# w2 phi2 with VectorE block turns in place of TensorE flips in five of eight chunks, in an attention, MoE and soft-MoE kernel on one core

## The chip, the cores and the metric

The kernel runs as one launch on one NeuronCore of a Trainium2 chip. The metric is the device time of one execution in microseconds, as the median of the runs. TensorE (PE) multiplies, VectorE (DVE), ScalarE (ACT) and GpSimd (POOL) work on elements, and SyncE (SP) issues every transfer between device memory and SBUF. All data are fp32; a part of the large products reads operands rounded to fp32r, split into a high and a low part.

## The reference

Attention over 32 memory slots, then a mixture of experts (`x` becomes `_moe_ref(...)`), then a soft mixture of experts. Cut to what the change touches:

```python
def _moe_ref(x, domain_probs, w1, w2):          # N=2304, D=512, E=4, F=1024
    for e in range(E):
        h = np.maximum(x @ w1[e], 0.0)
        out += p[:, e:e + 1] * (h @ w2[e])
    return out

def _moe2_ref(x, phi, w1, w2):                  # 8 experts, 32 slots
    logits = x @ phi                            # phi: 512 x 32
    d = softmax(logits, axis=0)
    slot_input = d.T @ x
    ...
```

The kernel never forms the output of the first mixture. It needs the 32 logits of each token, and h @ w2[e] @ phi = h @ (w2[e] phi). So it computes M = w2 phi2 once: for each of 4 experts a 1024 x 32 matrix, with `phi2` the 512 x 32 matrix of the second mixture.

## The kernel before, in words

The work is listed as steps. Each step has an engine, a planned cost, what it reads and writes, and a place `at` on a common scale. A planner (`Plan.order`) plays the steps through with those costs and writes one fixed order for each engine. On the chip every engine then takes its own list from the front, and a step waits for what it reads and for the places it overwrites. A step that waits holds up all that stands behind it on its engine.

The four batches are done in units: three units with 576 tokens of 4 heads by 2 halves each, and two half units for the last batch. Within a unit TensorE does, for 8 chunks of w1 (expert e, half f), `g_mult` (L695, folding w1 with the attention's values), 8 blocks of `up` (6 products each, L770 to L772, into one of three PSUM banks), and `logits` (L806, with M). ScalarE applies Relu (L778), VectorE turns the result in 32 x 32 blocks (L784) and GpSimd scales it (L788). Beside this the attention of the next batch is prepared (`memory`, `query`: L464 to L657).

`m_chunk(n, ats)` computes M for chunk n, which is one half of one expert's w2, 512 rows of 512. It is called for n = 0 to 7, all during the first unit. In the text "chunk 1" is n = 0 and "chunk 8" is n = 7. For each chunk:

- one transfer of 1 MB brings 512 rows of w2 into place `R[3 + n % 2]`, in runs of 8 KB (four rows to a partition);
- TensorE flips it in four groups of four 128 x 128 blocks (`flip`, L837), into a bank of `g_bank()`, which has two (4 and 5); ScalarE (L847) and VectorE (L843) copy the groups to SBUF in turn;
- four products of 128 x 32 by 128 x 512 (`part`, L854) with `phi2_sb` as weights, a copy by ScalarE (L860), and four products with the folding matrix `si` (`fold`, L866), which add the four parts; VectorE copies the result to M (L871).

`g_mult` takes the same two banks and gives them back when VectorE has done L706. Chunks with even n and odd n take turns in two places in SBUF, so a chunk's transfer waits for the reads of the chunk two before it.

Late in the kernel two TensorE steps load weights in steps of four elements: `slots` (L1249, `part[:, c::4]`) and the flip of the second mixture's h (L1292, `hs.rearrange("s (p f) -> s f p", f=4)[:, a_]`). They are of the kind of L866 and of L837, which load theirs in one run.

All transfers are issued by SP in one list. They use eight semaphores in turn, so a transfer is issued when the one eight before it has landed.

Of the kernel before, what the change touches and what calls it, by code (L numbers as in the profile page):

```python
# [11 lines left out]
PE, ACT, DVE, POOL, SP = "PE", "ACT", "DVE", "POOL", "SP"  # L12


class Plan:
# [16 lines left out]
    def add(self, eng, cost, fn, r=(), w=(), at=0.0, size=0, lag=LAG):  # L32
        self.stages.append((at, len(self.stages), eng, cost, fn, tuple(r), tuple(w), size, lag))
# [163 lines left out]
def dve(n):  # L197
    return 0.15 + 0.00107 * n
# [138 lines left out]
def program(  # L337
    tc, const, swap, ps, q, k, v, phi, dprob, w1, w2, phi2, v1, v2, out, nc, B, H, S, HD, NM, E, D, F, NSLOT, FH, NCH, SCALE, NT, HB, NG, ident, si, rr, r1, rf, ind, phi2_sb, dp, dps, pe, pe2, ct, kb, vb, kbs, vbs, M, srun, mrun, zrun, small, lts, lrs, lcs, dts, R, RAW, GP, AT, HT, NHT, PH, KT, QB, QT, XB, NX, YB, NY, MX, END, uses, h3, hts, atts, zone, z0, at_place, swapped, bank, MM, LB, S0, plan, **_
):
    add = plan.add  # L340

    def wk(o, n):
        return key("W", o, o + n)

    def pk(n):
        return key("ps", n)
# [7 lines left out]
    def g_bank():  # L354
        return uses(S0, S0 + 1)
# [11 lines left out]
    def dma(to, of, size, r=(), w=(), at=0.0, cost=0.6):  # L367
        add(SP, cost, lambda: nc.sync.dma_start(  # L368
            out=to() if callable(to) else to, in_=of() if callable(of) else of,
        ), r=r, w=w, at=at, size=size)  # L370
# [448 lines left out]
            r=[("M", n)] + [wk(o, width) for o in hos], w=[pk(LB)], at=at, lag=0)  # L819


    def m_chunk(n, ats):
        e, f = divmod(n, F // FH)
        o = R[3 + n % 2]

        def wn():
            return at_place(o, 2048).rearrange("p (a d) -> p a d", a=4)

        def wt():
            return at_place(o + 2048, 2048).rearrange("p (c f) -> p c f", c=4)  # L830
        dma(wn(), w2[e, f * FH:f * FH + FH, :].rearrange("(j a) d -> j a d", a=4), 1048576, w=[wk(o, 2048)], at=ats[0])
        for a in range(4):
            bk = g_bank()

            def flip(a=a, bk=bk):
                for c in range(4):
                    nc.tensor.transpose(  # L837
                        bank[bk][:, 128 * c:128 * c + 128], wn()[:, a, 128 * c:128 * c + 128], ident
                    )
            add(PE, 0.42, flip, r=[wk(o + 512 * a, 512), "cst"], w=[pk(bk)], at=ats[1 + a])  # L840
            src = bank[bk].rearrange("p (c f) -> p c f", c=4)
            if a % 2:
                add(DVE, dve(512), lambda a=a, src=src: nc.vector.tensor_copy(  # L843
                    out=wt()[:, :, 128 * a:128 * a + 128], in_=src),
                    r=[pk(bk)], w=[("wt", n % 2, a)], at=ats[1 + a] + 0.1)
            else:
                add(ACT, act(512), lambda a=a, src=src: nc.scalar.copy(  # L847
                    out=wt()[:, :, 128 * a:128 * a + 128], in_=src),
                    r=[pk(bk)], w=[("wt", n % 2, a)], at=ats[1 + a] + 0.1)
        bk = g_bank()  # L850

        def part():
            for c in range(4):
                nc.tensor.matmul(  # L854
                    bank[bk][32 * c:32 * c + 32, :], phi2_sb[:, c, :], wt()[:, c], start=True, stop=True,
                )
        wtk = wk(o + 2048, 2048)
        add(PE, 0.9, part, r=[("wt", n % 2, a) for a in range(4)] + [wtk, "phi2"], w=[pk(bk)], at=ats[5])
        mp = ct[:, 0:512]
        add(ACT, act(512), lambda: nc.scalar.copy(out=mp, in_=bank[bk]), r=[pk(bk)], w=["mp"],  # L860
            at=ats[5] + 0.1)
        b2 = g_bank()

        def fold():
            for a in range(4):
                nc.tensor.matmul(  # L866
                    bank[b2][:, 32 * a:32 * a + 32], mp[:, 128 * a:128 * a + 128], si,
                    start=True, stop=True,
                )
        add(PE, 0.95, fold, r=["mp", "cst"], w=[pk(b2)], at=ats[6])  # L870
        add(DVE, 0.3, lambda: nc.vector.tensor_copy(  # L871
            out=M[:, 4 * n:4 * n + 4], in_=bank[b2][:, 0:128].rearrange("p (a s) -> p a s", a=4),
        ), r=[pk(b2)], w=[("M", n)], at=ats[6] + 0.1)
# [272 lines left out]
    for x in range(4):  # L1146
        bk = att_bank()
        add(PE, 0.3, lambda x=x, bk=bk: spread(x, bk), r=["dpn", "cst"], w=[pk(bk)], at=2.5 + x)
        add(DVE, 1.1 if x == 3 else 0.5, lambda x=x, bk=bk: tables(x, bk), r=[pk(bk)], w=["pe"], at=2.6 + x)

    m_at = [2.5, 6.2, 10.5, 14.5, 18.5, 22.5, 26.5, 30.5]
    for n, m0 in enumerate(m_at):
        m_chunk(n, [m_at[n - 2] + 1.6 if n > 1 else n - 181.5, m0, m0 + 0.5, m0 + 1, m0 + 1.5, m0 + 2.4, m0 + 3.2])

    def attention(b, base):
        load_phi(b, base + 1)
# [8 lines left out]
    for u, (b, ranges) in enumerate(units):  # L1165
        if b + 1 < B:
            attention(b + 1, starts[u])
        for n in range(NCH):
            s = b * NCH + n
# [30 lines left out]
    for e in range(2):  # L1200
        def turn_s(e=e):
# [6 lines left out]
            at=z + 0.1)  # L1208
        x = sts[:, e]
        src = bank[so_b[e]].rearrange("p (k s) -> p k s", k=8)  # L1210
        w = [("M", n) for n in range(NCH)] if e == 0 else [("sts", 1)]
        if e:
            add(DVE, dve(512), lambda x=x, src=src: nc.vector.tensor_copy(out=x, in_=src), r=[pk(so_b[e])] + [("M", 7)],
                w=[("sts", e)], at=z + 0.2)
        else:
            add(ACT, act(512), lambda x=x, src=src: nc.scalar.copy(out=x, in_=src), r=[pk(so_b[e])],
                w=[("sts", e)] + [("M", n) for n in range(NCH)], at=z + 0.2)
# [25 lines left out]
    part = at_place(PART, 512)  # L1243
# [3 lines left out]
    def slots():  # L1247
# [7 lines left out]
        out=sT, in_=bank[b1][:, 0:128].rearrange("p (c s) -> p c s", c=4)  # L1255
# [11 lines left out]
    for m in range(4):  # L1267
        bu = end_mm()
        zz = z + 3 + 2 * m
        for n in range(4):  # L1270
# [15 lines left out]
            out=hs, in_=bank[bu], func=ACTF.Relu, scale=rz,  # L1286
# [28 lines left out]
    for e in range(8):  # L1315
        for nn in range(2):
# [9 lines left out]
            at = zz + 0.1 * (2 * e + nn)  # L1326
# [7 lines left out]
    for n, ab in enumerate(accs):  # L1334
        so, sk = sos[n]
        at = zz + 0.75 + n
        add(ACT, act(256), lambda ab=ab, so=so: nc.scalar.copy(out=so[:, 0:256], in_=bank[ab][:, 0:256]),
            r=[pk(ab)], w=[("so", n, 0), sk], at=at)
# [33 lines left out]
    at = zz + 3  # L1372
# [52 lines left out]
```

## Time and profile before

| | us |
|---|---|
| median of 3 runs | 508.97 |
| the runs | 508.2, 508.97, 511.94 |
| profiled execution | 507.71 |
| its span (first to last instruction) | 505.9 |
| TensorE busy in the span | 476.3 (94%) |
| VectorE, ScalarE, GpSimd busy | 297.1, 202.7, 212.1 |

The times in the trace are counted from the span's start. "Busy" is the time in which an engine has at least one instruction under way. On TensorE the products overlap (their ends are modelled), so that a group's busy time is smaller than its count times the mean of one. The weight loads (PEld) overlap with the products.

### The profile page before, as it was taken

What the parts mean: (1) busy time and instruction counts of PE and PEld (TensorE: products, weight loads), DVE (VectorE), ACT (ScalarE), POOL (GpSimd) and SP (SyncE); (2) the same over time, 40 slices, a digit from 0 to 9 for tenths busy, and PEclk for the clock granted to TensorE, in tenths of its full rate; (3) what the DMA queues carried; (4) which work ended last, traced back from release to release, by engine and by line L of the source; (5) the groups of instructions that cost most, each with busy time, mean ns of one, the idle gap of its engine ahead of it and who ended that gap; (6) DMA issues with size and microseconds to landing.
All of it is one profiled execution on the core that took longest, in us unless ns stands there. A gap on an engine that the chain in (4) does not pass through costs nothing.

```text
span 505.9 us, 13222 instructions
## 1 busy us (share of the span) xinstructions
PE 476.3 (94%) x5592; PEld 338.2 (67%) x5592; DVE 297.1 (59%) x605; ACT 202.7 (40%) x475; POOL 212.1 (42%) x255
## 2 busy tenths in 40 slices
PE   3999999999999999999999999999999989999971
PEld 2677787777876788788668887775687866333230
DVE  6588546656685857767684676586677553100032
ACT  2354445555550555455245555433543330010031
POOL 0244224546651348775324778532773850000000
PEclk9999999999999999999999999999999999899996
DMA  7999866415420946362082645525345988999938
GB/s 223 235 352 315 331 173 204 153 34 179 165 85 4 319 118 185 106 188 84 3 265 86 205 168 179 197 85 195 97 130 202 356 302 328 412 426 419 421 127 332
DMA packets 65243, 106.08 MB, mean 210 GB/s; under 512 B 28576, under 2 KB 40864, under 8 KB 59552
## 3 DMA queue, kind: packets, MB, share of 16 engines
q1 hardware_dynamic: 65184, 105.23, 60.9%
q8 instruction: 44, 0.72, 0.6%
q14 instruction: 15, 0.12, 0.1%
HBM read 100.50 MB, written 4.72 MB: 208 GB/s over the span
## 4 chain that ended last, share of the span: by engine, by line
PE 78%; DMA 14%; SPq 3%; DVE 2%; ACT 1%; issue 1%; DVEq 0%; ACTq 0%
PE ps L770 15%; PE ps L771 13%; PE ps L772 13%; PE ps L976 8%; DMA v<-in_moe_w_dram 8%; PE ps L695 6%; PE ps L806 5%; DMA h<-in_moe_w_dram 3%; PE ps L837 3%; SPq L368 3%; DMA raw<-in_moe_w_dram 3%; PE ps L813 2%; PE ps L854 2%; PE ps L603 2%; PE ps L615 2%; PE ps L866 1%
## 5 line engine op out<-in xcount | busy, mean ns | idle before, releaser
L788 POOL TENSOR_TENSOR h<-h,pe 128x576 f32<-128x576 f32 (+1 forms) x160 | 157.7, 996 | 141.5 <-DVE h L784 117.6
L770 PE MATMUL ps<-A,g 128*128 128x288 f32 x512 | 158.0, 309 | 0.2 <-ACT hts L778 0.2
L778 ACT ACTIVATE hts<-ps 128x288 f32<-128x288 f32 x256 | 105.1, 412 | 130.4 <-PE ps L772 129.0
L771 PE MATMUL ps<-A,g 128*128 128x288 f32 x512 | 151.1, 295 | 0.0
L772 PE MATMUL ps<-A,g 128*128 128x288 f32 x512 | 150.9, 295 | 0.0
L784 DVE STREAM_TRANSPOSE h<-hts 128x576 f32<-128x576 f32 (+1 forms) x160 | 102.4, 647 | 53.5 <-ACT hts L778 53.0
L770 PEld LDWEIGHTS ps<-A,g 128*128 128x128 f32 x512 | 96.1, 188 | 23.9 <-issue 18.6
L771 PEld LDWEIGHTS ps<-A,g 128*128 128x128 f32 x512 | 96.2, 188 | 0.3 <-POOL A L657 0.2
L772 PEld LDWEIGHTS ps<-A,g 128*128 128x128 f32 x512 | 96.1, 188 | 0.0
L706 DVE TENSOR_TENSOR g<-ps,g 128x512 fp32r<-128x512 f32 x64 | 41.0, 678 | 20.0 <-ACT g L704 19.9
L704 ACT CAST g<-ps 128x512 fp32r<-128x512 f32 x64 | 34.9, 590 | 34.5 <-PE ps L695 33.8
L976 PE MATMUL ps<-h,dts 32*32 32x512 f32 x1152 | 40.0, 597 | 1.6 <-DVE dts L958 1.6
L695 PE MATMUL ps<-raw,vbs 64*32 64x512 f32 x512 | 35.9, 600 | 1.6 <-DVE g L706 0.9
L976 PEld LDWEIGHTS ps<-h,dts 32*32 32x32 f32 x1152 | 22.8, 103 | 15.2 <-issue 4.6
L806 PE MATMUL ps<-hts,M 128*32 128x288 f32 x384 | 28.2, 411 | 0.0
L632 POOL TENSOR_TENSOR atts<-atts,small 128x256 f32<-128x256 f32 (+1 forms) x20 | 11.5, 575 | 25.7 <-DVE small L630 25.6
L837 PE MATMUL ps<-ident,h 128*128 128x128 f32 x128 | 18.1, 278 | 0.2 <-DVE g L706 0.2
L806 PEld LDWEIGHTS ps<-hts,M 128*32 128x32 f32 x384 | 10.4, 109 | 10.6 <-issue 5.1
L643 POOL TENSOR_TENSOR atts<-atts,small 128x256 f32<-128x256 f32 (+1 forms) x20 | 11.5, 575 | 13.4 <-DVE small L641 6.3
L837 PEld LDWEIGHTS ps<-ident,h 128*128 128x128 f32 x128 | 14.5, 143 | 2.4 <-issue 1.4
L894 POOL TENSOR_TENSOR lts<-lts,pe 128x288 f32<-128x288 f32 x15 | 10.4, 691 | 12.6 <-DMA v<-in_moe_w_dram 9.4
L657 POOL TENSOR_TENSOR A<-atts,A 128x256 fp32r<-128x256 f32 (+1 forms) x20 | 13.6, 680 | 4.4 <-ACT A L655 4.4
(185 smaller groups left out, 508.6 us busy)
## 6 DMA issues: line engine op xcount, KB each, us to landing
raw<-in_moe_w_dram SPq DMA_DIRECT2D x32, 1024.0 KB, 5.2
v<-in_moe_w_dram SPq DMA_DIRECT2D x20, 1024.0 KB, 12.5
h<-in_moe_w_dram SPq DMA_DIRECT2D x18, 1024.0 KB, 8.4
h<-in_k_dram SPq DMA_DIRECT2D x8, 512.0 KB, 5.2
h<-in_v_dram SPq DMA_DIRECT2D x8, 512.0 KB, 7.1
atts<-in_moe_w_dram SPq DMA_DIRECT2D x4, 1024.0 KB, 9.0
atts<-in_q_dram SPq DMA_DIRECT2D x12, 256.0 KB, 5.6
atts<-in_phi_dram SPq DMA_DIRECT2D x8, 256.0 KB, 4.7
```

Of the source, the lines that this page charges most:

```text
L695: nc.tensor.matmul(bank[bs[c]][32 * i:32 * i + 32, :], vb[b % 2][64 * c:64 * c + 64, 32 * i:32 * i + 32], t()[64 * c:64 * c + 64, i, :], s ...
L704: add(ACT, act(512), lambda c=c, src=src: nc.scalar.copy(out=placed(g()[:, 2 * c]), in_=src), r=[pk(bs[c])], w=[wk(o + 1024 * c, 512)], at ...
L706: add(DVE, dve(512), lambda c=c, src=src: nc.vector.tensor_tensor(out=placed(g()[:, 2 * c + 1]), in0=src, in1=placed(g()[:, 2 * c].bitcast ...
L770: nc.tensor.matmul(t, gh, ah, start=(c == 0), stop=False)
L771: nc.tensor.matmul(t, gh, al, start=False, stop=False)
L772: nc.tensor.matmul(t, gl, ah, start=False, stop=(c == 1))
L778: add(ACT, act(w), lambda: nc.scalar.activation(out=t[:, o0 - base:o1 - base], in_=bank[bm][:, 0:w], func=ACTF.Relu,), r=[pk(bm)], w=[wk(h ...
L784: add(DVE, dve(width), lambda: nc.vector.transpose(out=h_of(u, e)[:, kx], in_=t), r=[wk(ho, width)], w=[hk], at=at + 0.4)
L788: add(POOL, pool(width), lambda: nc.gpsimd.tensor_tensor(out=h_of(u, e)[:, kx], in0=h_of(u, e)[:, kx], in1=share, op=ALU.mult), r=["pe"], ...
L806: nc.tensor.matmul(lb[r0:r0 + 32, 0:HB], M[:, 4 * n + a, :], at_place(hos[a] + o0, o1 - o0), start=(first and h == 0), stop=(not first and ...
L837: nc.tensor.transpose(bank[bk][:, 128 * c:128 * c + 128], wn()[:, a, 128 * c:128 * c + 128], ident)
L976: nc.tensor.matmul(bank[S0 + p][32 * c:32 * c + 32, :], dtv[rows, tb, :], h_pair(u, ep)[rows, :, :, tb, :], start=(tb < 2), stop=(tb >= nt ...
```

## The change

Chunks 1 to 3 (n < 3) stay as they were. For chunks 4 to 8, `m_turned` takes the place of `m_chunk`:

- w2's half expert comes in four transfers of 256 KB, each into 32 partitions. A partition then has 8 rows' pieces of 256 columns, in runs of 1 KB.
- VectorE turns it in 32 x 32 blocks, four instructions of 128 x 512, SBUF to SBUF.
- TensorE does 32 small products (64 x 32 weights from a second copy of phi2, 64 x 128 of the turned w2): for c = 0 to 7 one in each of four 64 x 32 tiles of the array, added over c in PSUM.
- One VectorE turn of 128 x 128 from PSUM writes M.

The columns that a small product streams are read from SBUF in the order a, x, y of the layout `(y a c h x)`: y is innermost, and its two values lie 4 KB apart.

The second copy of phi2 (`load_phi2`) is four transfers of 32 KB in runs of 128 bytes. The flips of chunks 1 to 3 name the new transfers' keys as read, which orders them before the new transfers. The cost that the planner is given for the 32 products is 2.3.

```diff
+    def load_phi2(at):
+        for p in range(4):
+            dh = p % 2
+            dma(
+                lambda p=p: phi_of()[32 * p:32 * p + 32],
+                phi2[256 * dh:256 * dh + 256].rearrange("(c i) s -> i c s", i=32),
+                32768, w=[("phi2", p)] + ([wk(R[4] + 4096, 256)] if p == 0 else []), at=at,
+            )
+    def m_turned(n, ats):
+        e, f = divmod(n, F // FH)
+        o = R[3 + n % 2]
...
+        def wt():
+            return at_place(o + 2048, 2048).rearrange("p (y a c h x) -> p h c a x y", y=2, a=4, c=8, h=2)
+        for p in range(4):
+            fh, dh = divmod(p, 2)
+            src = w2[e, FH * f:FH * f + FH, 256 * dh:256 * dh + 256]
+            src = src.rearrange("(h x k) d -> h x k d", h=2, k=8)[fh]
+            dma(
+                lambda p=p: wn(0, 4)[32 * p:32 * p + 32].rearrange("p (k d) -> p k d", k=8), src,
+                262144, w=[("wn", o, p)] + ([wk(o, 2048)] if p == 0 else []), at=ats[0] + 0.001 * p,
+            )
+        for a in range(4):
+            add(DVE, dve(512), lambda a=a: nc.vector.transpose(
+                out=at_place(o + 2048 + 512 * a, 512), in_=wn(a, 1)),
+                r=[wk(o + 512 * a, 512)] + [("wn", o, p) for p in range(4)],
+                w=[wk(o + 2048 + 512 * a, 512)], at=ats[1 + a])
+        bk = g_bank()
+        def part():
+            for c in range(8):
+                for q in range(4):
+                    rows = slice(64 * (q // 2), 64 * (q // 2) + 64)
+                    nc.tensor.matmul(
+                        bank[bk][32 * q:32 * q + 32, 0:128], phi_of()[rows, c, :], wt()[rows, q % 2, c],
+                        start=(c == 0), stop=(c == 7),
+                    )
+        add(PE, 2.3, part, r=[wk(o + 2048, 2048), wk(R[4] + 4096, 256)] + [("phi2", p) for p in range(4)],
+            w=[pk(bk)], at=ats[5])
+        add(DVE, 0.3, lambda: nc.vector.transpose(
+            out=M[:, 4 * n:4 * n + 4].rearrange("p a s -> p (a s)"), in_=bank[bk][:, 0:128],
+        ), r=[pk(bk)], w=[("M", n)], at=ats[5] + 0.1)
...
+    load_phi2(6)
     m_at = [2.5, 6.2, 10.5, 14.5, 18.5, 22.5, 26.5, 30.5]
     for n, m0 in enumerate(m_at):
-        m_chunk(n, [m_at[n - 2] + 1.6 if n > 1 else n - 181.5, m0, m0 + 0.5, m0 + 1, m0 + 1.5, m0 + 2.4, m0 + 3.2])
+        (m_chunk if n < 3 else m_turned)(n, [m_at[n - 2] + 1.6 if n > 1 else n - 181.5, m0, m0 + 0.5, m0 + 1, m0 + 1.5, m0 + 2.4, m0 + 3.2])
```

How the engines' lists stand at three places, with the line numbers of each kernel (L843, L871 and L891 of before are L897, L925 and L945 after). VectorE, from the second pair of chunk 3's flips to chunk 5; `h_103` is the place of w2, `h_89` that of the experts' h. Before:

```order
L843 COPY h_103<-ps_97 128x4x128 x2
L541 TENSOR_SCALAR small<-ps_99 128x2
L542 RECIPROCAL small<-small 128x2
L549 TENSOR_SCALAR atts<-ps_98,small 128x64
L549 TENSOR_SCALAR atts<-ps_99,small 128x64
L784 STREAM_TRANSPOSE h_89<-hts 128x576
L871 COPY M<-ps_97 128x128
L891 STREAM_TRANSPOSE lts<-ps_95 128x288
```

VectorE at the same place after:

```order
L897 COPY h_103<-ps_97 128x4x128
L855 STREAM_TRANSPOSE h_103<-h_103 128x512 x2
L897 COPY h_103<-ps_97 128x4x128
L855 STREAM_TRANSPOSE h_103<-h_103 128x512 x2
...
L784 STREAM_TRANSPOSE h_89<-hts 128x576
L925 COPY M<-ps_97 128x128
L855 STREAM_TRANSPOSE h_103<-h_103 128x512
L945 STREAM_TRANSPOSE lts<-ps_95 128x288
```

The first turn of chunk 4, which waits for that chunk's four transfers, now stands between chunk 3's two copies; and the first turn of chunk 5 stands ahead of the logits' turn.

VectorE a little later, after: the turns of chunks 5 and 6, and the L706 that give back `g_mult`'s banks.

```order
L855 STREAM_TRANSPOSE h_103<-h_103 128x512 x2
L871 STREAM_TRANSPOSE M<-ps_96 128x128
L855 STREAM_TRANSPOSE h_103<-h_103 128x512 x3
L784 STREAM_TRANSPOSE h_89<-hts 128x576
L855 STREAM_TRANSPOSE h_103<-h_103 128x512 x2
L784 STREAM_TRANSPOSE h_89<-hts 128x576
L706 TENSOR_TENSOR g<-ps_97,g 128x512
L706 TENSOR_TENSOR g<-ps_96,g 128x512
```

The eight turns of chunks 5 and 6 stand ahead of those two L706, which stood behind copies of flips before.

TensorE, from chunk 3's fold (L866 before, L920 after) on. Before, the next chunk's flips begin there:

```order
L866 MATMUL ps_97<-si,ct 128x32 x4
L837 MATMUL ps_96<-ident,h_103 128x128 x4
L806 MATMUL ps_95<-hts,M 32x288 x8
L837 MATMUL ps_97<-ident,h_103 128x128 x4
```

After:

```order
L920 MATMUL ps_97<-si,ct 128x32 x4
L806 MATMUL ps_95<-hts,M 32x288 x8
L865 MATMUL ps_96<-h_103 32x128 x32
...
L865 MATMUL ps_97<-h_103 32x128 x32
L865 MATMUL ps_96<-h_103 32x128 x32
```

Chunk 4 is one block of 32 products behind the logits; chunks 5 and 6 are two blocks back to back, six blocks of `up` and one `g_mult` later.

SP, from chunk 1's and 2's transfers on (`128x2048` is a whole chunk, `32x8x256` a quarter of one). Before:

```order
L368 DMA h_103<-in_moe_w_dram 128x2048 x2
L368 DMA atts<-in_k_dram 64x4x64 x2
L368 DMA h_89<-in_k_dram 128x4x256
L368 DMA atts<-in_phi_dram 128x4x128 x2
```

After:

```order
L368 DMA h_103<-in_moe_w_dram 128x2048 x2
L368 DMA h_103<-in_moe_phi_dram 32x8x32 x3
L368 DMA atts<-in_phi_dram 128x4x128 x2
L368 DMA atts<-in_phi_dram 64x4x32 x2
L368 DMA h_103<-in_moe_phi_dram 32x8x32
L368 DMA atts<-in_k_dram 64x4x64 x2
```

The four small transfers of phi2 now stand ahead of the second batch's k.

## Rows read from the trace of the kernel before

**Rows 1.** Windows: busy time by engine, granted clock, DMA share, GB/s.
```profile
28.00:62.00 34.00, 33.78 (x347) 26.17 (x346) 25.00 (x59) 16.30 (x36) 11.96 (x14) 1.00 1.04 334
62.00:110.00 48.00, 47.86 (x521) 38.05 (x520) 28.49 (x55) 24.73 (x54) 21.19 (x23) 1.00 0.47 144
200.00:400.00 200.00, 198.66 (x2508) 150.99 (x2507) 137.62 (x268) 92.86 (x227) 116.44 (x143) 1.00 0.47 155
430.00:506.00 76.00, 60.03 (x407) 20.40 (x396) 11.71 (x29) 10.02 (x19) 0.00 (x0) 0.92 0.87 356
```
**Rows 2.** Chain that ended last, 396 to 506: start, us, what.
```profile
428.16 3.64 PE ps L1235 x33
431.80 16.00 DMA v<-in_moe_w_dram
```
**Rows 3.** Chain, 61.9 to 109.8: shares by line.
```profile
by line: PE ps L837 19.5%; PE ps L770 13.8%; PE ps L771 12.2%; PE ps L772 12.1%; PE ps L854 10.7%; PE ps L866 9.7%; PE ps L806 6.7%; PE ps L603 4.3%; PE ps L695 4.3%; PE ps L615 3.2%; ACT ct L860 1.2%; PE ps L514 1.2%; PE ps L519 0.5%; PE p
```
**Rows 4.** Chain, 74 to 92: start, us, what.
```profile
88.80 0.47 PE ps L615 x16
```
**Rows 5.** Weight loads by line: duration min/median/max in ns, form.
```profile
L866 PEld LDWEIGHTS ps<-si,ct x64: 186/192/192, 39.7 to 109.5; 128*128 128x128 f32 x64
L1249 PEld LDWEIGHTS ps<-si,atts x8: 308/329/329, 435.9 to 437.5; 128*128 128x128 f32 x8
L837 PEld LDWEIGHTS ps<-ident,h x128: 137/141/225, 33.3 to 105.3; 128*128 128x128 f32 x128
L1292 PEld LDWEIGHTS ps<-ident,lcs x8: 195/214/218, 448.8 to 461.1; 128*128 128x128 f32 x8
```
**Rows 6.** VectorE, 0 to 100, by line and shape: busy, mean ns, idle before.
```profile
L784 DVE STREAM_TRANSPOSE h<-hts 128x576 f32<-128x576 f32 x16 | 12.3, 772 | 8.4 <-ACT hts L778 8.3
L843 DVE COPY h<-ps 128x512 f32<-128x512 f32 x14 | 9.5, 681 | 5.4 <-PE ps L837 5.3
L706 DVE TENSOR_TENSOR g<-ps,g 128x512 fp32r<-128x512 f32 x10 | 6.4, 675 | 1.2 <-ACT g L704 1.1
```
**Rows 7.** Windows, 44 to 52.
```profile
44.00:48.00 4.00, 4.00 (x36) 2.69 (x29) 2.24 (x4) 1.15 (x3) 0.70 (x2) 1.00 1.15 226
48.00:52.00 4.00, 4.00 (x43) 3.25 (x41) 3.93 (x7) 2.73 (x7) 1.15 (x1) 1.00 1.04 416
```
**Rows 8.** SP's queue: the issue of chunks 3 and 4.
```profile
46.33 2.15 SPq L368 DMA_DIRECT2D h<-in_moe_w_dram  x2
```
**Rows 9.** Issues, 46.2 to 46.6 and 46.6 to 47.5: KB each, median us to landing.
```profile
h<-in_moe_w_dram SPq DMA_DIRECT2D x1, 1024.0 KB, 7.9
h<-in_moe_w_dram SPq DMA_DIRECT2D x2, 1024.0 KB, 8.8
```
**Rows 10.** Chain, 49 to 64: start, us, what.
```profile
51.17 0.13 PE ps L772
51.31 1.13 PE ps L695 x16
...
53.04 1.30 DVE g L706 x2
54.34 1.06 PE ps L837 x8
55.40 0.58 PE ps L514 x32
...
59.07 1.00 PE ps L854 x8
...
61.90 0.47 PE ps L837 x4
62.38 1.11 PE ps L806 x16
```
**Rows 11.** Window in which k and v come in runs of 1 KB.
```profile
168.00:171.00 3.00, 3.00 (x72) 1.79 (x74) 3.00 (x5) 1.81 (x7) 0.00 (x0) 1.00 0.97 321
```
**Rows 12.** Issues, 98.2 to 98.5 (64 partitions) and 108 to 109 (128 partitions).
```profile
atts<-in_q_dram SPq DMA_DIRECT2D x1, 128.0 KB, 2.8
...
atts<-in_q_dram SPq DMA_DIRECT2D x1, 256.0 KB, 2.9
```

More of the change, by code (lines that the diff above doesn't have):

```diff
@@ L819, in logits, with phi_of, wn @@
             r=[("M", n)] + [wk(o, width) for o in hos], w=[pk(LB)], at=at, lag=0)
+    def phi_of():
+        return at_place(R[4] + 4096, 256).rearrange("p (c s) -> p c s", c=8)
+    def load_phi2(at):
[9 more added lines that the diff above has]
+        o = R[3 + n % 2]
+        def wn(q, w):
+            return at_place(o + 512 * q, 512 * w)
+        def wt():
[27 more added lines that the diff above has]
+        ), r=[pk(bk)], w=[("M", n)], at=ats[5] + 0.1)
     def m_chunk(n, ats):
@@ L839, in flip @@
                     )
-            add(PE, 0.42, flip, r=[wk(o + 512 * a, 512), "cst"], w=[pk(bk)], at=ats[1 + a])
+            add(PE, 0.42, flip, r=[wk(o + 512 * a, 512), "cst"] + [("wn", o, p) for p in range(4)], w=[pk(bk)],
+                at=ats[1 + a])
             src = bank[bk].rearrange("p (c f) -> p c f", c=4)
```

## Prediction

> **What bounds the kernel now.** I read the windows first, then the chain of work that ended last, then the rows of the lines that the change takes away or resembles. From 28 us on TensorE is busy nearly without a break: 33.78 of 34 us, 47.86 of 48, 198.66 of 200 [rows 1]. The eight chunks lie in the first two of these windows. The DMA queues are full in the first (share 1.04) and half empty in the second (0.47). From 430 on the DMA is full again, and the chain passes at 431.80 from a TensorE step to the loads of the last weights [rows 1, 2]. Those loads wait for places that earlier TensorE work gives back, so I take a shift of TensorE by 110 us to arrive at the end one for one. What counts, then, is TensorE's work between 54 and 110 us, and any wait that is put into its list there.
>
> **What goes.** Between 61.9 and 109.8 (47.9 us) the chain holds the flips of five chunks, their products and their folds: 19.5% L837, 10.7% L854, 9.7% L866 and 1.2% waiting for the copy L860 [rows 3]. That is 41.1% of 47.9 = 19.7 us, 3.94 us a chunk, all of it on the path. The copies of ScalarE and VectorE that go were beside it and give nothing.
>
> **What comes on TensorE.** 32 products of fp32 are 64 instructions: the trace records two for each (L615: 16 for 8 products). The nearest row is L615, 128 streamed columns into 32-column tiles, four tiles in turn: 16 in 0.47 us, 29.4 ns each [rows 4]. So 64 take 1.9 us if the streamed columns cost no more than L615's, which lie in one run. Here each column lies 4 KB from the one before. No row shows a streamed operand read so, but two rows show weights read in steps of 16 bytes by the same engine from the same memory: 329 ns in place of 192 (L1249 and L866) and 214 in place of 141 (L1292 and L837) for 128 columns [rows 5], that is 137 and 73 ns more. With four tiles at work side by side, 64 instructions pay 64 x 73 / 4 = 1.2 us to 64 x 137 / 4 = 2.2 us more: 3.1 to 4.1 us. The stream could also be free of it, hence bounds of 1.9 and 4.1, and beyond for a rival below. I take 3.6, the middle of the two strided rows, since a read in steps is nearer to a read in steps than to one in a run. TensorE then saves 3.94 - 3.6 = 0.34 a chunk, **1.7 us** in all.
>
> The Trainium skill (SBUF — State Buffer, "Door 1: The DMA port swizzle") says that SBUF is read in lines of 16 bytes, that accesses that cross to a new line pay, and gives 4 fp32 as the step that is still free. The first half agrees with L1249; its free step of 4 fp32 does not, since that is L1249's very step, and the row decides.
>
> **What comes on the DMA.** Three things make chunk data later in the stretch where the queues are full.
> The second phi2 adds 131 KB in short runs ahead of the second batch's k. At the lowest rate in view, 226 GB/s [rows 7], it takes 0.6 us, at half of that (its runs are shorter) 1.2: I take 0.9.
> Chunk 3 landed at 46.33 + 7.9 = 54.2 [rows 8, 9], and its flips began at 54.34, just behind L706 [rows 10]. They now begin 0.8 us later.
> Chunk 4 was issued about 0.5 us behind chunk 3 and took 2 x 8.8 - 7.9 = 9.7, so it landed near 56.6 [rows 8, 9]. It shifts by 0.9, and its own megabyte comes in runs of 1 KB: at 321 GB/s 3.3 us [rows 11] in place of 2.5 at 416 [rows 7]. It also goes into 32 partitions at a time. A load of 128 KB into 64 partitions took 2.8 us, one of 256 KB into 128 took 2.9 [rows 12]: half the bytes, hardly less time. If narrow transfers run at half the rate a chunk takes 6.5. Most of those 2.8 us is the latency of a lone transfer, so I take 4.2, nearer the low end. Chunk 4 then lands at 56.6 + 0.9 + 1.7 = 59.2.
> The Trainium skill (SBUF — State Buffer, "Door 1: The DMA port swizzle") gives 189 GB/s for partitions 0 to 31 against 328 for 128. By that a chunk would take an estimated 5.5 us, and the end would come some 4 us later than in my sum; no run here shows that figure.
>
> **What comes on VectorE.** A turn of 512 costs 772 x 512 / 576 = 686 ns [rows 6], four a chunk, against two copies of 681 before. VectorE has the room: 28.5 of 48 us [rows 1]. The order is the trouble. The first turn of chunk 4 waits for that chunk's landing and stands ahead of chunk 3's second copy, which TensorE needs for chunk 3's products. 59.2 + two turns 1.37 + copy 0.68 = 61.3. TensorE asks for it at 59.07 [rows 10] + 0.8 = 59.9 and waits 1.4. **Lateness so far 2.2 us.**
> Next, chunks 5 and 6 run back to back into the two banks that `g_mult` uses, and its L706 stand behind all the turns of chunk 6. TensorE: chunk 3's products to the end of its fold 2.83 (61.90 - 59.07), logits 1.11, chunk 4 3.6, six blocks of `up` at 6 x 0.13 = 0.79, `g_mult` 1.13 and about 1 us of attention (L514 0.58 and its like) [rows 10]: 61.3 + 2.8 + 1.1 + 3.6 + 4.7 + 1.1 + 1.0 = 75.6. Data: behind chunk 4 come a block of w1 (3.0) and two chunks (8.4), so chunk 6 lands at 59.2 + 11.4 = 70.6; four turns 2.7, two L784 1.5, two L706 1.35 [rows 6]: 76.2. A wait of **0.6 us**, and none if the products are slower still.
> Chunks 7 and 8 have the same pattern once more, with the third batch's phi behind chunk 8 on SP and its maxima (L457) ahead of the L706. Bounds: nothing to 5 us; at 3.6 us a block TensorE comes late itself, and I take **0.2**.
>
> **Sum.** -1.7 + 2.2 + 0.6 + 0.2 = +1.3 us. The profiled execution took 507.71, so 509.0 for it; the median of the runs is 508.97, 1.26 above it, and I forecast for the median: **510.3**. The bounds with these causes (3.1 to 4.1 us a block, 3.3 to 5 us a chunk's load) give 506 to 514.
>
> **Rivals.**
> *The stream is free.* TensorE takes 1.9 us a block and saves 5 x 2.04 = 10.2. The L615 row speaks for it. It does not all come out: the lateness of 2.2 stays, TensorE reaches chunk 5 at 73.9 against 76.2 (2.3), and the last pair costs more, 2.5 between its ends. -10.2 + 2.2 + 2.3 + 2.5 = -3.2: 505.8, down to 501 if the second and third wait vanish.
> *Strided streams hinder one another.* Two of the four tiles read from each half of the partitions. If the extra time of two adds up in place of overlapping, a block pays 64 x 137 / 2 = 4.4 more, 6.3 in all: 5 x 2.36 = 11.8, + 2.2 = 14, 523. No row shows several strided reads at once. It makes the kernel slower by 1% from 4.5 us a block on (5 x 0.56 + 2.2 = 5).
> *Narrow transfers at half the rate* (6.5 us a chunk): lateness 4.5 at chunk 3, chunk 6's banks at 83 against 78 (5), 2 more later, -1.7: +9.8, 519. Halfway (5.4 us a chunk) it is some 514.
>
> **How the numbers follow.** Chances: the forecast 0.45, the free stream 0.28, hindered streams 0.12, narrow transfers 0.15. Within 1% (5.1 us, about what can be told from no change here) lie 504 to 514. Faster: a third of the free stream's cases and a few of the forecast's, 0.14. Slower: nearly all of the hindered streams, half of the narrow transfers, a few of the forecast's, 0.23. The same: 0.63. The range of 502 to 517 leaves out the free stream's best and most of the hindered streams.
>
> **What the profile after would show.** The new block's line on the chain: 3.6 us a block, 1.9 if the stream is free, over 4.5 if hindered. TensorE idle before chunk 3's products, by VectorE's copy, 1 to 2 us. A chunk's four transfers from first issue to last landing 4 to 5 us beside the latency. If TensorE at 28 to 110 us has no new idle time at all, the waits are wrong; if the block takes near 2 us as well, I am wrong by some 10 us on the fast side.

## The result, and the profile after

The kernel after the change takes 516.2 us (median of 4 runs, 514.11 to 517.08) against 508.59 for the kernel before (the three runs above and a fourth, 507.94 to 511.94). The ratio is 1.0137, with a 95% interval of 1.0115 to 1.0159. The profiled execution has a span of 515.3 us, 9.4 more than before.

The windows of the kernel after, which answer to [rows 1]; the columns are us, busy time of TensorE, its weight loads, VectorE, ScalarE and GpSimd, granted clock, DMA share, GB/s:

```profile
28.00:62.00 34.00, 29.20 (x258) 22.62 (x258) 25.13 (x54) 14.60 (x33) 12.57 (x15) 0.95 1.03 292
62.00:110.00 48.00, 41.92 (x682) 34.38 (x675) 27.72 (x54) 11.92 (x29) 10.96 (x11) 0.90 0.78 178
110.00:200.00 90.00, 90.00 (x1229) 69.76 (x1231) 63.59 (x112) 42.90 (x105) 48.99 (x51) 1.00 0.42 134
200.00:400.00 200.00, 198.66 (x2512) 151.02 (x2502) 138.93 (x271) 94.32 (x231) 115.07 (x138) 1.00 0.46 145
```

Nearly all of it happens between 28 and 110 us. TensorE is idle there for 4.80 + 6.08 us where it was idle for 0.22 + 0.14, and its clock, 1.00 before, is at the lower of its two levels (1.2 in place of 2.4 GHz) for parts of both windows. From 110 on TensorE's busy time is that of before (90.00 of 90 and 198.66 of 200 us in both), but for one step: a `g_mult` that starts 8.45 us later than before takes 1.00 us longer, first before, then after.

```profile
262.15 1.09 PE L695 MATMUL ps<-raw,vbs 64*32 64x512 f32 x16
```

```profile
270.60 2.09 PE L695 MATMUL ps<-raw,vbs 64*32 64x512 f32 x16
```

The chain says that the shift then arrives at the end one for one: the load of the last weights, at 431.80 before [rows 2], starts 9.41 us later.

```profile
441.21 15.93 DMA v<-in_moe_w_dram
```

The groups of the new work, from the page (busy us, mean ns; then idle time before it and what ended it), and the first block in the timeline:

```profile
L855 DVE STREAM_TRANSPOSE h<-h 128x512 f32<-128x512 f32 x20 | 12.8, 679 | 12.2 <-DMA h<-in_moe_w_dram 12.2
L865 PE MATMUL ps<-h 64*32 64x128 f32 x320 | 13.8, 341 | 5.4 <-DVE g L706 5.4
```

```profile
70.51 2.36 PE L865 MATMUL ps<-h 64*32 64x128 f32 x64
72.80 0.40 PE L770 MATMUL ps<-A,g 128*128 128x288 f32 x1
```

At the full clock a block takes 2.3 us (70.51 to 72.80), well under the 3.94 us a chunk that the prediction read for the work that it replaces [rows 3]. By these two figures TensorE saves 1.64 a chunk, 8.2 us in all; the 8.2 is worked out, not measured. The engine got what the change was for, and lost more to waiting. The chain of waits from 45 to 112 shows where (start, us, what):

```profile
48.16 11.02 DMA h<-in_moe_w_dram
59.18 0.14 issue
59.32 1.94 PE ps L890 x8
...
70.57 7.22 DMA h<-in_moe_w_dram
77.92 1.30 DVE h L855 x2
...
83.94 9.84 DMA h<-in_moe_w_dram
93.90 0.74 DVE h L855 x2
...
95.13 1.26 DVE h L855 x2
96.39 0.90 DVE atts L457
...
97.98 0.59 DVE g L706
98.61 5.77 PE ps L865 x128
```

Before, this chain was TensorE almost throughout [rows 3, 10]. Now it passes three times through a load of w2, and twice from the load through VectorE's turns before TensorE gets work. At 48.16 + 11.02 = 59.2 chunk 3 lands, a chunk whose own transfer the change left alone; it landed at 54.2 [rows 8, 9]. At 83.94 + 9.84 = 93.8 chunk 8 lands; VectorE has waited for it, turns it, and only then reaches the L706 at 97.98 that gives back a bank for the 32 products of chunk 7, which had been turned by 89.

The waits of 28 to 110 (engine, line, released by: total, times, longest):

```profile
DVE h L855 <- DMA h<-in_moe_w_dram: 12.2, 4, 4.9
...
PE ps L865 <- DVE g L706: 5.4, 2, 3.2
...
PE ps L890 <- DMA h<-in_moe_w_dram: 3.5, 1, 3.5
```

And the clock, in windows of 4 us:

```profile
56.00:60.00 4.00, 0.68 (x4) 0.71 (x5) 0.68 (x1) 0.23 (x1) 1.18 (x1) 0.79 1.14 210
60.00:64.00 4.00, 4.00 (x53) 3.33 (x53) 0.69 (x1) 0.86 (x2) 0.00 (x0) 0.50 1.04 282
```

TensorE was busy for 0.68 of 4 us while it waited for chunk 3, and in the next 4 us, all of them busy, it ran at half speed: eight instructions of flips took 1.94 (above) against 1.06 [rows 10].

**The account.** Idle time is 82 us less TensorE's busy time in 28 to 110; work lost to the clock is the sum, over 41 windows of 2 us, of busy time x (1 - granted clock). Before: 0.4 and 0.0. After: 10.9 and 6.0. So 10.5 + 6.0 - 8.2 = +8.3 us, against the 8.45 by which the `g_mult` above starts late; the other 1.0 of the 9.4 is that step's own, and why it takes longer stays open. So close a fit is partly luck. The same sum gives -6.6 for e11 below, whose trace has that `g_mult` 6.35 us earlier than before, but -5.5 for e2, -0.7 for e9 and -2.3 for e10, where it is 2.7 earlier, 1.6 later and 0.1 later. The sum is thus good to some 3 us, and what takes the rest in those three is not known.

### The profile page after: what moved, and what is told of

Its sections match the earlier page's. It is cut to its first block, busy times and chain, and to the rows that moved or that the text cites. A ratio compares the mean times of both kernels' runs of the same rounds, so it can differ in the third digit from the quotient of the medians.

```text
span 515.3 us, 13555 instructions
## 1 busy us (share of the span) xinstructions
PE 475.5 (92%) x5752; PEld 339.0 (66%) x5752; DVE 302.8 (59%) x615; ACT 193.3 (38%) x460; POOL 211.4 (41%) x255
## 4 chain that ended last, share of the span: by engine, by line
PE 70%; DMA 20%; SPq 3%; DVE 3%; ACT 1%; issue 1%; DVEq 0%; ACTq 0%
PE ps L770 13%; PE ps L772 12%; PE ps L771 12%; DMA h<-in_moe_w_dram 9%; PE ps L1030 8%; DMA v<-in_moe_w_dram 8%; PE ps L695 5%; PE ps L806 5%; SPq L368 3%; PE ps L603 2%; PE ps L615 2%; PE ps L813 2%; DMA atts<-in_phi_dram 2%; DMA h<-in_q_dram 2%; PE ps L514 1%; PE ps L890 1%
## 5 line engine op out<-in xcount | busy, mean ns | idle before, releaser
L706 DVE TENSOR_TENSOR g<-ps,g 128x512 fp32r<-128x512 f32 x64 | 41.1, 678 | 19.6 <-ACT g L704 19.6
L855 DVE STREAM_TRANSPOSE h<-h 128x512 f32<-128x512 f32 x20 | 12.8, 679 | 12.2 <-DMA h<-in_moe_w_dram 12.2
L865 PE MATMUL ps<-h 64*32 64x128 f32 x320 | 13.8, 341 | 5.4 <-DVE g L706 5.4
L806 PEld LDWEIGHTS ps<-hts,M 128*32 128x32 f32 x384 | 10.5, 109 | 9.9 <-issue 4.5
L865 PEld LDWEIGHTS ps<-h 64*32 64x32 f32 x320 | 12.0, 131 | 7.2 <-DVE g L706 5.9
```

Source lines behind the costliest of these rows:

```text
L706: add(DVE, dve(512), lambda c=c, src=src: nc.vector.tensor_tensor(out=placed(g()[:, 2 * c + 1]), in0=src, in1=placed(g()[:, 2 * c].bitcast ...
L806: nc.tensor.matmul(lb[r0:r0 + 32, 0:HB], M[:, 4 * n + a, :], at_place(hos[a] + o0, o1 - o0), start=(first and h == 0), stop=(not first and ...
L865: nc.tensor.matmul(bank[bk][32 * q:32 * q + 32, 0:128], phi_of()[rows, c, :], wt()[rows, q % 2, c], start=(c == 0), stop=(c == 7),)
```

## The experiments

Every kernel was compared with the kernel before on the same chip, where that one's median was 508.59 to 509.79; e1 to e4 ran on one chip, e5 to e8 on a second, e9 to e11 on a third, e12 on a fourth. Between rows of different chips the ratios are what to compare. "Idle" and "clock" are the two sums just explained. e1 to e5 and e11 time the work alone: their data or weights are not those that M needs.

| kernel | median us | ratio, 95% interval | idle | clock |
|---|---|---|---|---|
| after | 516.20 | 1.0137, 1.0115 to 1.0159 | 10.9 | 6.0 |
| e1: wide transfers, four | 506.45 | 0.9935, 0.9911 to 0.9958 | 4.9 | 1.7 |
| e2: wide transfer, one | 507.21 | 0.9949, 0.9931 to 0.9968 | 3.1 | 0.0 |
| e3: columns from one run | 515.55 | 1.0114, 1.0086 to 1.0142 | 12.9 | 4.2 |
| e4: kernel before, narrow loads | 511.38 | 1.0034, 1.0015 to 1.0054 | 3.2 | 1.4 |
| e5: no second phi2 | 513.92 | 1.0090, 1.0058 to 1.0122 | 10.2 | 4.8 |
| e8: chunks 6 to 8 only | 514.95 | 1.0111, 1.0082 to 1.0141 | 8.7 | 3.4 |
| e9: planner told the load's rate | 510.58 | 1.0025, 1.0004 to 1.0047 | 5.0 | 2.9 |
| e10: chunks 4, 6, 8 only | 508.52 | 0.9993, 0.9976 to 1.0010 | 3.0 | 0.0 |
| e11: wide and no second phi2 | 502.21 | 0.9869, 0.9835 to 0.9904 | 2.0 | 0.0 |
| e12: e9, phi2 copied on chip | 511.09 | 1.0023, 1.0004 to 1.0043 | 5.5 | 3.4 |

e6 (two transfers of 64 partitions, 604.59 us) and e7 (two queues, 517.89) stand below.

My theory after the result: the narrow loads are too slow for TensorE's new pace, and VectorE's list passes their lateness on to chunks that are ready. Rivals: the number of transfers, the block of products, the second phi2.

**e1 and e2: width or number of transfers.**

```diff
-            src = src.rearrange("(h x k) d -> h x k d", h=2, k=8)[fh]
+            src = src.rearrange("(x k) d -> x k d", k=2)
-                lambda p=p: wn(0, 4)[32 * p:32 * p + 32].rearrange("p (k d) -> p k d", k=8), src,
+                lambda p=p: wn(p, 1).rearrange("p (k d) -> p k d", k=2), src,
```

(e1: the same four transfers of 256 KB in runs of 1 KB, each into 128 partitions; its fh and dh then pick a quarter of the rows and columns. e2 has one transfer of 1 MB in runs of 8 KB.)

> The changed kernel with each chunk's four transfers still of 256 KB in runs of 1 KB, but each into all 128 partitions in place of 32 (the blocks then lie elsewhere, so M is computed from misplaced data). Narrow transfers as the cause (a quarter takes 1.27 us in the changed kernel's trace, 5.1 us a chunk): a quarter takes 0.8 to 0.9 us, chunk 3's flips wait under 1.5 us, TensorE keeps its fast clock, 503 to 506 us. Number of transfers as the cause (four issues and four of the eight semaphores a chunk): no change, 514 to 517. VectorE's order as the cause: 511 to 515.

> The changed kernel with one transfer of 1 MB a chunk in runs of 8 KB into 128 partitions, as chunks 1 to 3 have it (M from misplaced data). Narrow transfers or number of transfers as the cause: 501 to 505 us, since TensorE saves 5 x (3.94 - 2.3) = 8.2 us and little of it is given back. VectorE's order as the cause (the first turn of chunk 4 ahead of chunk 3's second copy, the turns of chunks 5 and 6 ahead of L706): TensorE still waits 2 us or more at each, 508 to 515.

e1 is 9.7 us faster than the kernel after and faster than the kernel before; e2, with one transfer and long runs, is no faster than e1. So neither the number of transfers nor the 1 KB runs matter much: the width does. The DMA's own rows show it. First the kernel after, 68.6 to 71, then e1, 69.5 to 73.5, both while quarters land (packets, MB, rate; then the queue's share of 16 engines):

```profile
DMA packets 603, 0.49 MB, mean 205 GB/s; under 512 B 154, under 2 KB 603, under 8 KB 603
...
q1 hardware_dynamic: 603, 0.49, 112.6%
```

```profile
DMA packets 1156, 1.13 MB, mean 282 GB/s; under 512 B 69, under 2 KB 1155, under 8 KB 1155
...
q1 hardware_dynamic: 1155, 1.11, 91.4%
```

With the engines full, the narrow form moves 205 GB/s, 5.1 us a chunk; the wide one moves 282 with room left, 3.7 us. The first stretch has more small packets of other loads (154 of 603 under 512 B, against 69 of 1156), so a count by size is cleaner: from 55 to 110 us each trace records 5120 packets of 1024 bytes, all of w2 (before has none there), and one takes a median of 85 ns in the kernel after and 46 in e1. The lists of all five engines are the same in the two traces. TensorE's rows of e1, 62 to 110:

```profile
62.00:110.00 48.00, 46.89 (x759) 38.43 (x758) 34.11 (x64) 17.17 (x41) 17.75 (x19) 1.00 0.64 192
```

1.1 us idle in place of 6.1, and the clock full.

**e3: the stream's stride.**

```diff
-            return at_place(o + 2048, 2048).rearrange("p (y a c h x) -> p h c a x y", y=2, a=4, c=8, h=2)
+            return at_place(o + 2048, 2048).rearrange("p (h c n) -> p h c n", h=2, c=8)
```

> The changed kernel with the 128 columns of each small product streamed from one run in place of steps of 4 KB (M from misplaced data); all else as it is. If steps cost, the block at full clock falls from 2.3 to 1.9 us; if not, it stays at 2.3. Late data as the cause: the time stays within 1.5 us of the changed kernel, 514 to 517, because TensorE waits anyway. The stream as the cause: 2 to 3 us faster.

```profile
L865 PE MATMUL ps<-h 64*32 64x128 f32 x320 | 9.3, 270 | 3.6 <-DVE g L706 3.6
```

In one run a block takes 9.3 / 5 = 1.87 us and an instruction 270 ns; with columns 4 KB apart it is 2.3 and 296. The stride costs 0.4 a block. The whole kernel gains nothing that can be told (515.55): 2 us less of products became 2 us more of idle time (12.9), since the loads set the pace.

**e4: narrow loads in the kernel before.** Chunks 4 to 8 with the flips as they were, loaded by the four narrow transfers.

```diff
-        dma(wn(), w2[e, f * FH:f * FH + FH, :].rearrange("(j a) d -> j a d", a=4), 1048576, w=[wk(o, 2048)], at=ats[0])
+        for p in range(4 if n >= 3 else 0):
...
+                lambda p=p: at_place(o, 2048)[32 * p:32 * p + 32].rearrange("p (k d) -> p k d", k=8), src,
+                262144, w=[("wn", o, p)] + ([wk(o, 2048)] if p == 0 else []), at=ats[0] + 0.001 * p,
```

> The kernel before with its flips, products and folds for all chunks, but chunks 4 to 8 loaded by the four transfers of 256 KB into 32 partitions (M from misplaced data). The transfers as the cause, narrow or many: TensorE idles for chunk 3's or later flips and the kernel is 3 to 10 us slower than before, 512 to 519. VectorE's order, the turns or the small products as the cause: the time of before, 507 to 510.

Only 0.34% slower (1.7 us). One wait, before chunk 3's flips, is all; behind it TensorE is never short:

```profile
62.00:110.00 48.00, 47.94 (x532) 38.22 (x528) 28.08 (x58) 23.25 (x51) 19.23 (x21) 1.00 0.80 170
```

So narrow loads alone don't explain 7.6 us. The likely reason, which this run doesn't test by itself: with flips a chunk takes TensorE 3.94 us, and a wait for a load stands in TensorE's own list. With turns a chunk takes 2.3, and the wait stands in VectorE's list, ahead of work that other chunks need.

**e5 and e11: the second phi2.**

```diff
-                        bank[bk][32 * q:32 * q + 32, 0:128], phi_of()[rows, c, :], wt()[rows, q % 2, c],
+                        bank[bk][32 * q:32 * q + 32, 0:128], phi2_sb[rows, c % 4, :], wt()[rows, q % 2, c],
...
-    load_phi2(6)
```

> The changed kernel without the second copy of phi2: its four small transfers are gone and the 32 products take rows of the first copy as weights (wrong weights, the same work). If those transfers (1024 runs of 128 bytes each way ahead of chunk 3) are what made chunk 3 land at 59.2 in place of 54.2, chunk 3's flips begin near 55.5 in place of 59.3, the turns of chunk 4 come 2 to 4 us earlier, and the time falls from 516 to about 512 to 513. If chunk 3 is late because SP issues it late or because the queues are shared otherwise, its flips stay at 58 to 59.5 and the time at 515 to 516.5.

> Both suspects taken out at once: chunks 4 to 8 in four transfers of 256 KB into all 128 partitions (which puts the data elsewhere than the products want them) and no second copy of phi2 (wrong weights). If narrow loads and the phi2 transfers are the two causes and add up, the time is 506.45 - 2.3 = about 504, and TensorE's saving of 8.2 us comes out but for 3 to 4 us. If the phi2 transfers matter only beside narrow loads, it stays at 506 to 507.

Without it the kernel after gains 2.3 us (by the two intervals some 0.4 to 4.4). e1 gains 4.2 by the medians (506.45 to 502.21), but 3.4 by the ratios, as the two ran on different chips; the 2.3 of e11's first theory lies within the error of that. The chains give when chunk 3 is issued and how long it takes to land, in e5, e1, e11 and, for narrow loads without a second phi2, e4:

```profile
47.99 9.01 DMA h<-in_moe_w_dram
```

```profile
49.18 8.82 DMA h<-in_moe_w_dram
```

```profile
46.63 8.69 DMA h<-in_moe_w_dram
```

```profile
47.32 9.68 DMA h<-in_moe_w_dram
```

Chunk 3 is late by 5.0 us after the change (54.2 to 59.2): it is issued 1.8 later (48.16 against 46.33) and takes 3.1 longer (11.02 against 7.9). Of the 3.1, taking away the second phi2 gives back 2.0 (e5), making the loads behind chunk 3 wide gives back 2.2 (e1), and both together 2.3 (e11): the two causes don't add up here. The 1.8 can't be shared out. e4, e5 and e11 have the same list for SP up to the issue of chunk 3, that of the kernel before, and yet issue it at 47.32, 47.99 and 46.63. As e5 also brings back that list, in which the loads `h<-in_k` stand ahead of a block of w1 again, the bytes of phi2 and the order that came with them are not told apart. e11 shows what the change is worth without both: 6.5 us faster than before.

**e9: the order alone.** The loads stay narrow; only the size that the planner is given for them grows. All engines then get a new order: VectorE's list as expected below, but TensorE's too (chunks 5 and 6, and 7 and 8, are no longer back to back), and SP issues chunk 8 behind a load of the third batch's phi.

```diff
-                262144, w=[("wn", o, p)] + ([wk(o, 2048)] if p == 0 else []), at=ats[0] + 0.001 * p,
+                450000, w=[("wn", o, p)] + ([wk(o, 2048)] if p == 0 else []), at=ats[0] + 0.001 * p,
```

> The changed kernel's loads as they are, but the planner is told 1.36 us for each quarter (close to the 1.25 to 1.3 us between landings in its trace) in place of 0.79. VectorE's list then has chunk 3's second copy ahead of the first turn of chunk 4, and two L706 ahead of half the turns of chunk 6; the work is the same. If the coupling through VectorE's list carries most of the loss, TensorE no longer waits for chunk 4's landing at chunk 3's products and the time falls by 3 to 5 us, to 511 to 513. If the load itself is too slow for TensorE's pace, the wait only moves to the 32 products and the time stays at 514 to 517.

510.58: one number gives back 5.6 us. The gain lies in one window. TensorE in 80 to 110, first after, then e9:

```profile
80.00:110.00 30.00, 23.92 (x413) 20.55 (x412) 17.85 (x34) 7.20 (x19) 9.05 (x9) 0.89 0.72 167
```

```profile
80.00:110.00 30.00, 29.27 (x499) 23.33 (x495) 20.56 (x40) 11.03 (x28) 12.40 (x15) 1.00 0.84 174
```

And VectorE's timeline in that stretch, again after and e9:

```profile
93.90 2.49 DVE L855 STREAM_TRANSPOSE h<-h 128x512 f32<-128x512 f32 x4 [4.87 <-DMA h<-in_moe_w_dram]
96.32 0.98 DVE L457 TENSOR_REDUCE atts<-atts 128x128 f32<-128x512 f32 x1
...
97.90 0.65 DVE L706 TENSOR_TENSOR g<-ps,g 128x512 fp32r<-128x512 f32 x1
```

```profile
92.69 1.28 DVE L706 TENSOR_TENSOR g<-ps,g 128x512 fp32r<-128x512 f32 x2
...
98.45 0.71 DVE L855 STREAM_TRANSPOSE h<-h 128x512 f32<-128x512 f32 x1 [1.86 <-DMA h<-in_moe_w_dram]
```

In e9 the bank for chunk 7 comes back before VectorE waits for chunk 8, although chunk 8 itself lands later than it did. I had expected the gain at chunk 3's products; there nothing changed (48 to 62: 10.78 busy against 10.47). This shows that the planned order carries more than half of the loss, given narrow loads, and e1 that the loads carry all of it, given the order: the loss needs both. That VectorE's part of the order does it is what the two timelines suggest; no run changes VectorE's list alone.

**e8 and e10: fewer chunks turned.** e8 turns chunks 6 to 8 only, and loads phi2 later; e10 turns chunks 4, 6 and 8, with e9's size and phi2 between chunks 1 and 2.

The line of e10:

```diff
-        (m_chunk if n < 3 else m_turned)(n, [m_at[n - 2] + 1.6 if n > 1 else n - 181.5, m0, m0 + 0.5, m0 + 1, m0 + 1.5, m0 + 2.4, m0 + 3.2])
+        (m_turned if n in (3, 5, 7) else m_chunk)(n, [m_at[n - 2] + 1.6 if n > 1 else n - 181.5, m0, m0 + 0.5, m0 + 1, m0 + 1.5, m0 + 2.4, m0 + 3.2])
```

> Only chunks 6 to 8 are turned; chunks 4 and 5 keep their whole transfer and their flips, and the second copy of phi2 is loaded later. Two blocks fewer give back 2 x 1.64 = 3.3 us of TensorE's saving (8.2 in all for five). If the narrow loads and VectorE's order cost mostly at chunks 3 to 6, the waits of about 5 us at chunk 3 and some of the 5 at chunk 6 go and the time is 508 to 511. If they cost the same wherever the first turned chunk stands, it is 513 to 516.

> Only chunks 4, 6 and 8 are turned; chunks 5 and 7 keep their whole transfers and flips; the second copy of phi2 is loaded between chunks 1 and 2; the planner is told 1.36 us a quarter. Three blocks save 3 x 1.64 = 4.9 us on TensorE. Two chunks in a row then need 5.1 + 2.5 = 7.6 us of load in place of 10.2. If slow loads back to back are the cause, most waits behind chunk 4 go and the time is 507 to 510; if a single narrow load already makes TensorE wait by itself, it is 511 to 515.

e8 moved the waits and kept most of them (8.7 us of idle time); of its two cases the second came, 513 to 516. e10 is level with the kernel before, 508.52 to 508.68: the clock stays full and the idle time is 3.0. By the account it should be 2.6 - 4.9 = -2.3; the profiled span is the same as before (505.9), so 2.3 us are open there, as much as in e9; 0.6 of them may lie ahead of 28 us, where TensorE's busy time in 0 to 28 is 17.94 in place of 18.54.

**e6 and e7: other ways to load the same bytes.** e6 uses two transfers of 512 KB into 64 partitions, e7 issues the last two of the four transfers from ScalarE.

```diff
+        for p in range(2):
+            src = w2[e, FH * f + 256 * p:FH * f + 256 * p + 256].rearrange("(x k) (j d) -> j x k d", k=8, j=2)
```

```diff
+            else:
+                add(ACT, 0.1, lambda p=p, src=src: nc.scalar.dma_start(
```

> The changed kernel with each turned chunk loaded by two transfers of 512 KB into 64 partitions each, in place of four of 256 KB into 32; the same bytes, the same runs of 1 KB, the same places. If the width of a transfer sets its rate, a chunk takes about 3.0 to 3.6 us in place of 5.1, TensorE's waits before chunks 4 and 6 shrink by about 2 us each, and the time is 507 to 510. If only transfers into all 128 partitions are quick, 64 partitions take about 4 to 5 us a chunk and the time is 512 to 515. If the loss is VectorE's order alone and not the load, it stays at 515 to 517.

> The changed kernel with the last two of each chunk's four transfers issued by ScalarE, so that they can run beside the first two. If a 32-partition transfer is slow because of the partitions that it writes, two at a time into other partitions overlap, a chunk takes 2.6 to 3.5 us and the time falls to 508 to 512, less what ScalarE loses by waiting for the places. If the 16 DMA engines are slowed by the narrow packets themselves, nothing overlaps and it stays at 515 or above; a ScalarE that waits in its list would make it slower still, up to 520.

e6 took 604.59 us, which no theory had. Its window from 64 to 76, when the two transfers of chunk 4 are nearly alone:

```profile
64.00:76.00 12.00, 0.00 (x0) 0.00 (x0) 0.00 (x0) 0.00 (x0) 0.00 (x0) 0.61 0.14 47
```

A share of 0.14 is about 2 of 16 engines (0.125): the pattern's outermost dimension is j, with two values, and it seems that each value went to one engine. So e6 says nothing on the width of 64. e7 (1.0176, 1.0147 to 1.0206) shows no overlap of narrow transfers into different partitions: in 76 to 80 two queues together move 173 GB/s at a share of 1.05. A third of the packets there are small, but those of 1024 bytes take a median of 81 ns (55 to 110 us), hardly less than the 85 with one queue. It also puts waits into ScalarE's list. The 1.7 us that it is slower than the kernel after are within the two intervals.

**e12: what the runs pointed to.** e9 with the second phi2 made on the chip by 16 products with the identity.

```diff
+        add(PE, 0.7, move, r=["cst", "phi2"], w=[pk(bk)], at=at)
+        add(ACT, act(256), lambda: nc.scalar.copy(
+            out=phi_of().rearrange("p c s -> p (c s)"), in_=bank[bk][:, 0:256]),
...
-    load_phi2(6)
+    copy_phi2(-163.8)
```

> The version that the runs point to, nothing left out: chunks 4 to 8 turned, the planner told 1.36 us a quarter, and the second copy of phi2 made on the chip near 30 us by 16 small products with the identity (estimated at about 0.5 us of TensorE, from 29 ns an instruction of L615) and one copy by ScalarE, in place of four transfers. If the phi2 transfers cost 2.3 us here as they did in the changed kernel, the time is 510.6 - 2.3 + 0.5 = 508.8, level with the kernel before, or up to 2 us faster where the waits at chunk 3 go. If narrow loads keep TensorE waiting at chunk 3 and 4 anyway, it is 510 to 512.

511.09, no gain over e9. Chunk 3's flips came early, but the planner again set the first turn of chunk 4 ahead of chunk 3's second copy, and TensorE waited there and ran slowly behind it:

```profile
61.75 0.71 DVE h L861
62.46 0.59 DVE h L903
63.18 1.07 PE ps L914 x8
64.25 0.54 PE ps L770
```

This is the wait that the prediction had at that place (the copy L903, then chunk 3's products L914). No version with the whole computation beats the kernel before; e10 equals it.

## Why the prediction was right and wrong, step by step

The time lies in the range, 5.9 us above the forecast and 0.8 below the upper end; it is above the 506 to 514 that the prediction gave for the causes in its sum. The likeliest case, no change, did not happen; the rival of narrow transfers did, near its halfway point (514 at 5.4 us a chunk; 5.1 was measured). Its terms:

| step of the prediction | forecast | measured |
|---|---|---|
| block of 32 products | 3.6 (1.9 to 4.1) | 2.3 |
| TensorE's saving, five chunks | 1.7 | 8.2, worked out with the same 3.94 |
| a chunk's load | 4.2 (3.3 to 6.5) | 5.1 |
| second phi2, chunk 3 later by | 0.9 | 2.0 of its landing, with SP's order (e5) |
| chunk 3's flips later by | 0.8 | 5.0 |
| wait at chunk 3's products | 1.4 | none there |
| L706 behind chunk 6's turns | 0.6 | 2.2 |
| last pair | 0.2 (0 to 5) | 3.2, and what led to it |
| lower clock | not in the sum | 6.0 |

**The block failed first.** I took strided weight loads [rows 5] as the nearest rows for a strided stream. e3 shows that the stream pays 0.4 a block, not 1.7. L615's row [rows 4] was the better guide: 1.9 against e3's 1.87. The free stream was nearly true, and yet its time, 505.8, is not what came.

**The loads.** "Nearer the low end" was wrong: 205 GB/s. The Trainium skill's figure, which the prediction set beside its sum (SBUF — State Buffer, "Door 1: The DMA port swizzle": 189 GB/s for partitions 0 to 31, 328 for 128), agrees with these rows in direction, 205 and 282.

**Chunk 3's lateness** was mis-sized most. The prediction counted phi2 by bytes and a halved rate, and nothing for chunks 3 and 4 sharing the queues. The chain shows 11.02 us from issue to landing against 7.9 [rows 9], and 9.7 in e4, where only the narrow loads share the queues with it; the issue itself came 1.8 later, which the prediction did not count. With the flips 5 us late the wait at chunk 3's products vanished: VectorE's copy was done at 66.4 and TensorE, slow by then, came at 66.6. e12, where the flips were early, has it.

**The L706.** Both places were named, and both waits came, the second well above its 0.2, inside its bound of 5. I had let TensorE be late itself at 3.6 us a block; at 2.3 it was early and the wait stood in full. e9, where these L706 come earlier in a new order of all lists, is 5.6 us faster.

**The 3.94** holds 1.2% of the chain, 0.1 us a chunk, that stood for the wait on the copy L860; TensorE was idle for only 0.14 us in that whole stretch, so this part was not TensorE's time to save.

**The clock** was missing. A sum of waits alone treats TensorE as fast as before after each of them; here 10.5 us of idle time brought 6.0 of slow work.

Two large errors of opposite sign, a saving too small by 6.5 and waits with the clock too small by 13.5 (10.5 + 6.0 against 2.2 + 0.6 + 0.2), leave 7.0 of the 8.1 us by which the profiled execution came out above its forecast (517.08 against 509.0); another 1.0 is the slow `g_mult` at 270.60. The median came out 5.9 above. The mechanism of the waits was right in kind and in two of its three places, but the range held by luck as well: with the waits and the clock as measured and the saving as forecast, the time would have been some 524, outside it.

## What to carry to other kernels

Before work moves from one engine to another, price the loads in the form that the new work wants: here the narrow form took some 40% more time than the wide one for the same bytes (5.1 against 3.7 us), and the faster consumer only made its waits longer. Where an in-order engine waits for a load, list what stands behind the waiting instruction and who needs that; an order in which two L706 stand ahead of the wait was 5.6 us faster at no change of the work. When an order is planned from costs, give the plan the measured cost of a load: e9 changed nothing else.

## What the runs showed of the hardware

- Transfers into 32 partitions move 205 GB/s at full queues, where the same sizes and runs into 128 partitions move 282; a packet of 1024 bytes takes a median of 85 ns in place of 46 (after and e1). Issuing half of them from a second queue did not help (e7: 173 GB/s, 81 ns). The Trainium skill (DMA: Bandwidth & Descriptors, "Rules for kernel authors") says that transfers to disjoint partition halves serialize, and e7 agrees; why a narrow packet is slower, no run here settles.
- A transfer whose pattern begins with a dimension of two used about two of 16 engines, 47 GB/s, and cost the kernel 95 us (e6). The same section of the Trainium skill states that rule: the outermost dimension bounds the number of engines.
- In the kernel after TensorE was busy for 0.68 us of 56 to 60, and its granted clock stood at the lower of its two levels, 0.50 (1.2 GHz), through the whole of 60 to 64, in which it was never idle. In e2, e10 and e11, with 2 to 3 us of idle time between 28 and 110, the clock did not fall there; in e4, with 3.2 us, 2.5 of them in one wait, it did.
- A streamed operand with neighbours 4 KB apart costs 296 ns for 128 columns against 270 in one run, much less than strided weights (329 against 192 [rows 5]).
